# An adaLN transformer block on one core: attention outputs written straight to where the projection reads them, head sets in pairs, and a table of moves over the planned order

## The chip, the cores and the metric

One Trainium2 chip, of which the kernel uses one core. The metric is device time in microseconds (us). A core has five engines with an instruction queue each: TensorE (PE, with its weight loads shown apart as PEld), VectorE (DVE), ScalarE (ACT), GpSimd (POOL) and SyncE (SP, which here issues nearly all DMAs).

## The reference

```python
# x [1, 2048, 640], c [1, 640], bf16; 32 heads of 20; F = 1536
mod = (silu(c) @ w_mod).reshape(1, 6, 1, 640)
sa, ca, ga, sb, cb, gb = mod[:, 0], ..., mod[:, 5]
h = layernorm(x) * (1 + ca) + sa
qkv = (h @ wqkv)                       # 640 -> 3 * 640
p = softmax(q @ k.T * 20 ** -0.5)      # 2048 x 2048 for each head
x = x + ga * ((p @ v) @ wo)            # 640 -> 640
h = layernorm(x) * (1 + cb) + sb
x = x + gb * (((h @ w_gate) * (h @ w_up)) @ w_down)
```

## The kernel before

**A planner writes the program.** The Python code creates some thousand tasks (a group of matmuls, one exponential, one DMA, ...), each with its engine, an assumed duration, a priority, the tasks it depends on and the buffers it must acquire. A list scheduler (`Sched`) runs them against assumed costs and so fixes one order for each of the queues of PE, DVE, ACT, POOL and SP. `emit_program` then writes these orders out with semaphores. On the chip nothing is reordered: each engine goes through its list and waits where a semaphore isn't there yet.

**Tiling.** The 2048 queries are cut in 7 chunks (`CHUNKS`: one of 512, six of 256), the 32 heads in 8 sets of 4 (`NSET`). A pair of chunk and set is an *item*. An item's scores are made in *units* of 512 columns, keys on the partitions; there are 2048 units in all. A *score visit* of PE (line 1524, `ps_all<-QT,KT`) makes two units, with matmuls that use one of four 32-row strips of the array each (a head of a set lies on each strip), into a pair of PSUM banks; there are two such pairs of banks. For most units one ACT instruction (line 1561, `PP<-ps_all`, 1024 columns) takes the exponential of both units into a buffer `PP`. For the units that the table `QUADS` names, in fours, DVE makes it from integer operations on the bits of a bf16: line 1585 (`DB<-ps_all`) takes a unit out of PSUM, lines 1617 and 1625 (`DSS<-DB`) make two terms of four units, and their product is made by DVE (line 1622) or by POOL in four pieces (line 1637).

**PV and the end of an item.** The PV matmuls (line 2192, `ps_all<-PP,Vf` and `<-DSS,Vf`, 128x32 column strips, one strip for each head) sum an item's output in one PSUM bank, 21 columns a head: the sum of the exponentials and 20 outputs. When an item is through, line 1717 (DVE) transposes the bank in 32x32 blocks into `OT`, line 1723 (DVE) takes reciprocals into `invT`, line 1725 (POOL, for the last sets DVE) multiplies, all 32 columns of each head's band, into `OTn`, line 1734 (DVE) transposes back into `OcT`, and strip DMAs of line 1746 on SP (248 issues, 10 KB each as a rule) copy the 20 rows of each head from their bands of 32 to where the output projection wants them, `Ocp` (640 rows as five blocks of 128). The last set of the last chunk is projected from `OcT` itself, with a small copy of its part of w_o, `wo7`.

**The rest of a chunk** is its *suffix*: output projection, residual and LN2, then for each of 12 blocks of 128 of F a gate and an up product (line 970, `ps_all<-h2T,stg`; their weights are loaded anew for each chunk into buffers `stg`) that share one bank, 256 columns each, a copy of the gate half to `gsb` (line 1959; ACT or DVE), the product of both (line 1997, `hprod`), and the down-projection (line 970, `ps_all<-wd,hprod`). The suffix of a chunk is woven between the scores of the next ones, its places set by fractions (`GATE_F`). Fill matmuls (line 2523) stand where PE's planned work is thin.

**The start.** LayerNorm, transposes (copies at line 1133) and the projections to Q, K and V. K and Q go out to DRAM and come back in the layout with one head per 32-row strip: line 1289 (`KT<-k_rows`) and line 1298 (`QT<-q_rows`), on SP. w_o comes early in one DMA, `wo7` in four (line 1493). The later sets' K and Q are projected during the first sets' scores.

The end of an item, cut to the operations:

```python
t1: e.transpose(OT[:, 0:n], ps[:, bank, 0:n]...)                      # DVE, line 1717
t2: e.reciprocal(invT[:, 0:nb32]..., OT[...][:, :, 0:1])              # DVE, line 1723
t3: e.tensor_tensor(OTn[:, 0:n]..., OT[:, 0:n]..., invT..., ALU.mult) # POOL or DVE, line 1725
t4: e.transpose(OcT[:, s, 0:n], OTn[:, 0:n])                          # DVE, line 1734
for (b5, s, r0, nr, ro) in pcs:                                       # SP, line 1746
    e.dma_start(Ocp[r0:r0 + nr, slot, b5, qo:qo + n],
                OcT[32 * s + 1 + ro:32 * s + 1 + ro + nr, s_, 0:n])
```

Of the kernel before, what the change touches and what calls it, by code (L numbers as in the profile page):

```python
# [13 lines left out]
SEM = 60.0  # L14
# [4 lines left out]
X_FIRST = 0.0  # L19
ACT_LAT = 250.0  # L20
# [16 lines left out]
LKTOL = 300.0  # L37


class Task:  # L40
    __slots__ = ("head", "hval", "hknow", "eng", "dur", "lat", "deps", "emits", "ctr", "prio", "gate", "acq", "on_start", "slots",
                 "start", "done", "needed", "val", "know", "nleft", "ready", "users", "name", "mode", "seq", "rt", "sem",
                 "nbytes", "cond", "alt", "land", "firm", "lk", "dead", "key")

    def __init__(self, eng, dur, emits, deps=(), ctr=None, prio=0.0, lat=None, gate=0, acq=(), on_start=None,
# [28 lines left out]
        self.dead = False  # L74
        if lat is None:
            lat = {"pe": PE_DRAIN, "act": ACT_LAT, "dve": DVE_LAT, "pool": 60.0}.get(eng, 0.0)
        self.lat = lat

# [5 lines left out]
class Slots:  # L84

    def __init__(self, ids, name=""):
        self.name = name
        self.free = [(i, []) for i in ids]
        self.hold = {}
        self.gone = set()  # L90
        self.out = {}

    def avail(self, only=None):
        best = None
        for k, (i, rel) in enumerate(self.free):
            if only is not None and i != only:
                continue
            t = 0.0
            for r in rel:
                t = max(t, r.done + SEM)  # L100
            if best is None or t < best[0]:
                best = (t, k)
        return best
# [13 lines left out]
    def done(self, i, task):  # L117
        h = self.hold[i]
# [9 lines left out]
    def add(self, i, rel):  # L128
        self.free.append((i, rel))


class Sched:

    def __init__(self):
# [28 lines left out]
        self.lk_last = None  # L163

# [39 lines left out]
    def _enable(self, task):  # L204
        t = 0.0
        for d in task.deps:
            t = max(t, d.done + SEM)
# [70 lines left out]
    def step_engine(self, eng):  # L278
        if self.free_at[eng] > self.t:
            return False  # L280
        self.pull(eng)
        rl = self.readyl[eng]
        for k, task in enumerate(rl):
# [5 lines left out]
            if self.locked(eng, task):  # L289
                continue  # L290
            if self.acquire(task, self.t):
# [63 lines left out]

def emit_program(nc, sched, nsem_dma=56):
# [23 lines left out]
    for t in sched.all:  # L380
# [11 lines left out]
        for d in deps:  # L392
            if not (d.nbytes or d.eng != eng or d.eng in ("dve", "pool")):
                continue
            if d.head and eng == "act":
# [85 lines left out]
QUADS = ((0, 4, 3, 3, 3, 4, 4, 4), (2, 2, 1, 2, 2, 2, 1, 2), (2, 2, 1, 2, 2, 2, 1, 2), (2, 2, 1, 2, 2, 2, 1, 2), (2, 2, 1, 2, 2, 2, 1, 2), (2, 2, 1, 2, 2, 2, 1, 2), (2, 1, 2, 2, 2, 1, 2, 0))  # L481
SPLITJ = 1
QHALF = ((0, 0), (0, 0))
TB_GATE = 2
# [3 lines left out]
D_LEAD = 0.451  # L488
NB0, NSS = 3, 3
XB0, XSS = 0, 0  # L490
HEADG = 1000
OP_EARLY = 1
EV_OP = 0.5
# [3 lines left out]
LN2T = 0.6  # L497
# [5 lines left out]
HOLD = 110  # L503
PVTOL = 249
XDPRIO = 1.343
# [5 lines left out]
STX_G, STX_T, STX_S, W_ISSUE = 3, 20, 1.5, 600.0  # L511
ZFILL = 1
WD_POOL, WD_PRIO = 1, 400.0
# [4 lines left out]
WM_GATE = 8  # L518
# [3 lines left out]
K_LEAD = 0.683  # L522
# [3 lines left out]
D_LATE = 16  # L526
D_RES = 20
PVMIN, PVMAX, PVCAP = 2, 7, 12
PV0 = 0
V_PARTS = [[0, 2], [2, 4], [4, 6], [6, 8]]  # L530
V_L1 = 0.2
# [10 lines left out]
GATE_F = (0.446, 0.5, 0.5, 0.5, 0.5, 0.5, 1.0)  # L542
FILL_MIN = 4190.746
# [9 lines left out]
LN2P = 0.85  # L553
NALT = 1
OPFIRST = 1500
STG_B = 0.95
ENDP, END3, P_POW = 0.4, 1, -1.0
HT_L = 0.25
V_L = 0.221
LATE_A = 2.065  # L560
LATE_L = 1.418
LATEQ = (2, 3)
LATEQ_A = -20
LATEQ_F = 0.35
# [4 lines left out]
    0: {"PVMIN": 2, "HOLD": 95, "PVTOL": 249, "D_RES": 58, "PVCAP": 6, "X_HALF": 0.0, "XDPRIO": 1.343, "FILL_MIN": 3463.3, "LKTOL": 300.0, "EAGER": 9, "PVMAX": 14, "X_LATE": -179.96, "TPRIO": 0.75, "STEAL_GAP": 200, "D_LATE": 16, "PV_KEEP": 2},  # L569
    1: {"PVCAP": 15, "XBACK": 1, "FILL_MIN": 4629.7},  # L570
    2: {"DL": 0.376},
    4: {"HOLD": 58.0, "X_LATE": -39.3},
    5: {"D_LATE": 7, "PVMAX": 3},
    6: {"X_LATE": 168.4, "FILL_MIN": 5225.9, "HOLD": 156.4},
    7: {"DL": 0.501},
    8: {"FILL_MIN": 2868.8},
    10: {"X_HALF": 69.3, "HOLD": 73.7, "PVMAX": 5},
    11: {"DL": 0.443},
    12: {"DL": 0.459, "HOLD": 108.3, "X_LATE": 6.6},
    13: {"DL": 0.417},  # L580
    15: {"X_LATE": 86.8},
    16: {"HOLD": 135.0, "FILL_MIN": 4362.5},
    17: {"X_LATE": -17.4, "LKTOL": 338.9, "HOLD": 52.0},
    19: {"DL": 0.471, "PVMAX": 7, "HOLD": 113.6},
    20: {"DL": 0.391, "PVMAX": 10},
    21: {"X_LATE": -85.4, "PVMIN": 3},
    24: {"DL": 0.464, "STEAL_GAP": 210.6, "X_LATE": -52.5, "PVCAP": 14, "HOLD": 116.4, "LKTOL": 98.1},
    25: {"DL": 0.549, "LKTOL": 370.4, "HOLD": 156.3},
    26: {"DL": 0.411, "PVMIN": 1, "X_LATE": 2.0, "EAGER": 6, "X_HALF": 58.0},
    27: {"DL": 0.473},  # L590
    29: {"HOLD": 148.6, "D_LATE": 5, "LKTOL": 267.5, "D_RES": 36, "PVMAX": 3},
    30: {"EAGER": 11},
    31: {"X_LATE": -99.6, "HOLD": 173.2, "X_HALF": 164.9, "PV_KEEP": 2},
    33: {"DL": 0.442, "PVMIN": 7, "PV_KEEP": 3, "X_HALF": 147.4},
    34: {"PVMIN": 3, "X_HALF": 26.9, "STEAL_GAP": 91.8, "EAGER": 8, "X_LATE": 136.8, "D_RES": 25},
    35: {"X_HALF": 148.7},
    36: {"DL": 0.524},
    37: {"FILL_MIN": 4112.0, "EAGER": 8, "X_LATE": -201.5},
    39: {"STEAL_GAP": 162.9, "EAGER": 9},
    42: {"PVMAX": 8, "FILL_MIN": 4334.4, "PV_KEEP": 3},  # L600
    43: {"HOLD": 127.6},
    46: {"D_LATE": 20, "PV_KEEP": 3, "X_LATE": -80.9},
    53: {"LKTOL": 820.1, "X_HALF": 73.5},
    54: {"PVTOL": 279.6, "FILL_MIN": 4011.5, "X_HALF": 31.3},
}
XHALF = 1
STG_G0, STG_G, XC_G = 12, -10, -20
X_LATE = -24.052
X_HALF = 0.0
# [10 lines left out]
def build_kernel(nc, A_x, A_wqkv, A_wo, B_x, B_w_gate, B_w_up, B_w_down, c, w_mod, out):  # L620
# [96 lines left out]

    PPs = [alloc("PP", [128, NPS, w * 512], BF16) for w in ((3, 2) if HEADG < 1000 else (2, 2))]
    wo7 = alloc("wo7", [128, D], BF16)
# [9 lines left out]
    OTn = alloc("OTn", [128, 512], BF16)  # L729
    NOC = 2  # L730
    OcT = alloc("OcT", [128, NOC, 512], BF16)
    oc_off = region(2 * KD * 512 * 2)
    Ocp = at("Ocp", [128, 2, KD, 512], BF16, oc_off)
# [6 lines left out]
    late_off = region(late_size)  # L740
    early_off = region(early_size)
    R1 = Sub(late_off, late_size)
# [4 lines left out]
    R1 = Sub(early_off, early_size)  # L747
# [5 lines left out]
    R2 = Sub(early_off, early_size)  # L753
    hprod = R2.alloc("hprod", [128, FT, 512], BF16)
    h2T = R2.alloc("h2T", [128, KD, 512], BF16)
    xck = R2.alloc("xck", [128, 4, D], BF16)
    xn2 = R2.alloc("xn2", [128, 4, D], BF16)
# [8 lines left out]
    KPB = alloc("KPB", [128, 2, 512], BF16)  # L766
# [30 lines left out]
    G = Slots([5, 6, 2, 7], "G")  # L797
    GX = Slots([3, 4] if HEADG else [2, 3, 4], "GX")
    hx = (1, 3) if HEADG else (1, 3, 4)
    GC = Slots([0, 1], "GC")  # L800
    setA = Slots([0], "A")
    setB = Slots([0], "B")
    pPs = [Slots(list(range(NPS)), "PP") for _ in range(2)]

    def ring():
        return len(pPs[0].free) + len(pPs[1].free)
# [3 lines left out]
    sOcT = Slots(list(range(NOC)), "OcT")  # L810
# [407 lines left out]
    def k_base(tc):  # L1218
        return 80 if tc in K_DIRECT else 0
# [87 lines left out]
    def v_round(t, pt, prio, gate=0):  # L1307
        a, z = V_PARTS[pt]
        nh = 4 * (z - a)
        w = nh * DH  # L1310
        mms = []
        for k in range(KD):
            f = quarters(w, lambda k=k: hT[t // 4][:, k, t % 4 * 128:t % 4 * 128 + 128],
                         lambda k=k: wV[:, k, 80 * a:80 * a + w], k == 0, k == KD - 1)
            mms.append((X(w), f))

        def after(r):
            dst = Vf[:, (t * H + 4 * a) * VW:(t * H + 4 * a + nh) * VW].rearrange("p (h w) -> p h w", w=VW)[:, :, 1:VW]
            f = lambda e: e.tensor_copy(dst, ps[:, r.b["b"], 0:w].rearrange("p (h w) -> p h w", w=DH))
# [1309 lines left out]
```

## Time and profile before

| | |
|---|---|
| median of 3 runs | 804.14 us (803.36 to 807.19) |
| profiled execution: span | 803.8 us (0.3 under the median) |
| first exponential starts, last one starts | 16.35 us, 774.7 us |
| DMA over the span | 64.66 MB, mean 80 GB/s |

The profile is one execution of the program, recorded by the hardware; times in it are microseconds from the start of its span. "L1561" is line 1561 of the kernel. A group's row reads: line, engine, operation, output <- inputs, partitions x elements, number of instructions, then busy time, mean ns of one, idle time of the engine before them and what ended it. A row of a wait reads: who waited, on what, for whom, total us, number of waits, longest wait. Matmuls are pipelined and their ends are modelled, so PE's busy time isn't PE at its peak.

### The profile page before, as it was taken

What the parts mean: (1) busy time and instruction counts of PE and PEld (TensorE: products, weight loads), DVE (VectorE), ACT (ScalarE), POOL (GpSimd) and SP (SyncE); (2) the same over time, 40 slices, a digit from 0 to 9 for tenths busy, and PEclk for the clock granted to TensorE, in tenths of its full rate; (3) what the DMA queues carried; (4) which work ended last, traced back from release to release, by engine and by line L of the source; (5) the groups of instructions that cost most, each with busy time, mean ns of one, the idle gap of its engine ahead of it and who ended that gap; (6) DMA issues with size and microseconds to landing.
All of it is one profiled execution on the core that took longest, in us unless ns stands there. A gap on an engine that the chain in (4) does not pass through costs nothing.

```text
span 803.8 us, 37761 instructions
## 1 busy us (share of the span) xinstructions
PE 790.4 (98%) x16595; PEld 380.6 (47%) x16595; DVE 697.8 (87%) x1401; ACT 764.8 (95%) x847; POOL 386.0 (48%) x396
## 2 busy tenths in 40 slices
PE   8999999999999999999999999999999999999998
PEld 4433433333244434445555455555555555555567
DVE  7978788799989999988999999999899988898754
ACT  6899899999999999999999999999999999999961
POOL 3347455654366565763444443545534554455300
PEclk9999999999999999999999999999999999999999
DMA  9733212212341532120032404231540254414420
GB/s 297 243 113 91 62 43 64 61 33 76 92 109 50 167 88 52 35 55 13 24 81 65 95 16 112 57 73 39 121 89 15 54 118 94 98 37 106 92 68 18
DMA packets 154314, 64.66 MB, mean 80 GB/s; under 512 B 116951, under 2 KB 154151, under 8 KB 154151
## 3 DMA queue, kind: packets, MB, share of 16 engines
q1 hardware_dynamic: 153223, 61.10, 30.0%
q8 instruction: 132, 2.16, 1.1%
q10 hardware_dynamic: 928, 1.15, 0.5%
q14 instruction: 31, 0.25, 0.1%
HBM read 50.63 MB, written 8.99 MB: 74 GB/s over the span
## 4 chain that ended last, share of the span: by engine, by line
PE 77%; ACT 14%; DVE 5%; issue 2%; DMA 1%; SPq 1%; POOL 0%; DVEq 0%; ACTq 0%
PE ps_all L1524 26%; PE ps_all L970 21%; PE ps_all L2192 19%; ACT PP L1561 14%; PE ps_all L1230 4%; PE ps_all L966 3%; DVE DB L1585 2%; PE ps_all L1889 1%; PE ps_all L1166 1%; PE ps_all L1127 1%; DVE DSS L1617 1%; PE ps_all L2523 0%; DVE DSS L1625 0%; DMA QT<-q_rows 0%; PE ps_all L991 0%
## 5 line engine op out<-in xcount | busy, mean ns | idle before, releaser
L1561 ACT ACTIVATE PP<-ps_all 128x1024 bf16<-128x1024 f32 x810 | 748.5, 1090 | 6.7 <-PE ps_all L1524 4.8
L1637 POOL TENSOR_TENSOR DSS<-DB,DSS 128x512 bf16<-128x512 bf16 x268 | 305.0, 1157 | 290.6 <-DVE DSS L1625 254.2
L1585 DVE TENSOR_SCALAR DB<-ps_all 128x512 int16<-128x512 f32 x428 | 285.5, 681 | 50.5 <-PE ps_all L1524 48.0
L1524 PE MATMUL ps_all<-QT,KT 32*128 32x256 bf16 (+2 forms) x3648 | 319.4, 287 | 4.5 <-DMA QT<-q_rows 0.8
L1524 PEld LDWEIGHTS ps_all<-QT,KT 32*128 32x128 bf16 x3648 | 93.9, 92 | 204.1 <-ACT PP L1561 141.5
L2192 PE MATMUL ps_all<-PP,Vf 128*32 128x256 bf16 (+2 forms) x2892 | 163.6, 291 | 0.5 <-DVE KPB L1242 0.3
L970 PE MATMUL ps_all<-h2T,stg 128*32 128x256 bf16 (+2 forms) x2716 | 122.9, 281 | 0.3 <-DVE DB L1585 0.2
L2192 PEld LDWEIGHTS ps_all<-PP,Vf 128*32 128x32 bf16 (+1 forms) x2892 | 54.5, 94 | 76.4 <-issue 67.6
L2192 PE MATMUL ps_all<-DSS,Vf 128*32 128x256 bf16 (+1 forms) x1512 | 88.7, 291 | 0.0
L1617 DVE TENSOR_SCALAR DSS<-DB 128x2048 int16<-128x2048 int16 x107 | 77.2, 722 | 0.8
L970 PEld LDWEIGHTS ps_all<-h2T,stg 128*32 128x32 bf16 x2716 | 61.6, 96 | 26.9 <-issue 22.0
L1625 DVE TENSOR_SCALAR DSS<-DB 128x2048 int16<-128x2048 int16 x107 | 73.2, 684 | 0.8 <-PE ps_all L2192 0.8
L970 PE MATMUL ps_all<-wd,hprod 128*32 128x320 bf16 (+1 forms) x1404 | 61.0, 277 | 0.0
L1725 POOL TENSOR_TENSOR OTn<-OT,invT 128x256 bf16<-128x256 f32 (+1 forms) x49 | 35.3, 721 | 37.7 <-DVE invT L1723 37.5
L1622 DVE TENSOR_TENSOR DSS<-DB,DSS 128x2048 bf16<-128x2048 bf16 x40 | 51.5, 1287 | 0.0
L2192 PEld LDWEIGHTS ps_all<-DSS,Vf 128*32 128x32 bf16 x1512 | 36.5, 95 | 20.9 <-issue 12.4
L970 PE MATMUL ps_all<-wV,hT 128*32 128x160 bf16 x1280 | 38.9, 236 | 0.9 <-DVE DB L1585 0.3
L970 PEld LDWEIGHTS ps_all<-wd,hprod 128*32 128x32 bf16 x1404 | 31.2, 96 | 14.2 <-issue 10.8
L1717 DVE STREAM_TRANSPOSE OT<-ps_all 128x256 f32<-128x256 f32 (+2 forms) x57 | 27.1, 475 | 8.8 <-PE ps_all L2192 8.5
L1230 PE MATMUL ps_all<-hT,wk 128*32 128x512 bf16 x360 | 32.3, 382 | 0.0
L970 PEld LDWEIGHTS ps_all<-wV,hT 128*32 128x32 bf16 x1280 | 24.6, 97 | 15.9 <-issue 8.2
L1230 PE MATMUL ps_all<-hT,wq 128*32 128x512 bf16 x375 | 31.3, 382 | 0.6 <-DVE OT L1717 0.6
(133 smaller groups left out, 556.1 us busy)
## 6 DMA issues: line engine op xcount, KB each, us to landing
stg<-in_B_w_gate_dram SPq DMA_DIRECT2D x74, 160.0 KB
stg<-in_B_w_up_dram SPq DMA_DIRECT2D x74, 160.0 KB
KT<-k_rows SPq DMA_DIRECT2D x112, 32.0 KB
QT<-q_rows SPq DMA_DIRECT2D x48, 64.0 KB
Ocp<-OcT SPq DMA_DIRECT2D x164, 10.0 KB
wm<-in_w_mod_dram SPq DMA_DIRECT2D x3, 800.0 KB
x<-in_A_x_dram SPq DMA_DIRECT2D x7, 320.0 KB
k_rows<-KPA SPq DMA_DIRECT2D x16, 128.0 KB
```

The costliest lines, as they stand in the source:

```text
L970: return lambda e, b: e.matmul(ps[32 * x:32 * x + 32, b, c0 + o:c0 + o + w], lhs()[:, 32 * x:32 * x + 32], rhs() if w == n else rhs()[:, o ...
L1230: f = [lambda e, b_, k=k, x=x: e.matmul(ps[x:x + min(32, w - x), b_, :], wx[:, k, r0 + x:r0 + min(x + 32, w)], hT[tc][:, k, :], tile_posit ...
L1524: ems.append(lambda e, i=i, kt=kt: e.matmul(dstf()[:, i * u.n:(i + 1) * u.n], KT[32 * u.s:32 * u.s + 32, u.j, kt * 128:(kt + 1) * 128], QT ...
L1561: return e.activation(PPs[g % 2][:, cellp["p"], 0:nu * 512], ps[:, b0:b0 + nu, :].rearrange("p b c -> p (b c)"), AFT.Exp, scale=ESCALE)
L1585: return e.tensor_scalar(DBl[st_["slot"]][:, x * 512:(x + 1) * 512], bank(cell["b"]), EBIAS, 0.0, op0=ALU.add, op1=ALU.max)
L1617: return e.tensor_scalar(DSl[st_["ss"][0]][:, :], DBl[st_["slot"]][:, :], 0x7F, 0x3F00, op0=ALU.bitwise_and, op1=ALU.bitwise_or)
L1622: return e.tensor_tensor(d, DBl[st_["slot"]][:, :].bitcast(BF16), d, ALU.mult)
L1625: return e.tensor_scalar(DSl[st_["ss"][1]][:, :], DBl[st_["slot"]][:, :], 0x7F80, 2, op0=ALU.bitwise_and, op1=ALU.bitwise_or)
L1637: return e.tensor_tensor(d, DBl[st_["slot"]][:, x * w:x * w + w].bitcast(BF16), d, ALU.mult)
L1717: t1 = Task("dve", n * 1.1 + 70, lambda e: e.transpose(OT[:, 0:n], ps[:, item_info[it]["bank"], 0:n].rearrange("p (b q r) -> p b r q", q=3 ...
L1725: f3 = lambda e: e.tensor_tensor(OTn[:, 0:n].rearrange("p (b c r) -> p b r c", c=32, r=2), OT[:, 0:n].rearrange("p (b r c) -> p b r c", c= ...
L2192: ems.append(lambda e, i=i, kt=kt, stt=stt, stp=stp: e.matmul(ps[32 * s:32 * s + mc, bk, 0:u.n], Vf[:, (kt * H + 4 * u.j + s) * VW:(kt * H ...
```

## The change

1. **Outputs straight to `Ocp`.** The multiply keeps 20 columns of each head, not 32, and puts them beside each other in a buffer `OTn` that holds the outputs of all eight sets of a chunk, so that the 160 columns of a partition group fill five bands of 32. The second transpose then goes from `OTn` to `Ocp`, for those bands that the set has filled. `OcT`, the 248 strip DMAs and `wo7` are gone. Since each strip of `Ocp` now holds the heads in another order, the rows of w_o are permuted, by 48 DMAs of 4 to 20 rows (line 1898 of the changed kernel) in place of one and four.
2. **Pairs.** For chunks of 256 queries two head sets (even and odd) share one PSUM bank in PV, 256 columns each; lines 1717 and 1723 then run once for both, over 512 columns.
3. **Gate and up.** A bank holds two gate blocks or two up blocks, not one of each: the copy to `gsb` and the product run over 512 columns, half as often. Two more `stg` buffers (`MORE = 2`).
4. **Score visits.** Which units share a visit is chosen while the planner runs, among the next six (`LOOK = 6`), so that they lie on different strips; `PP` is one ring of 16 slots, and the exponential may write two slots that don't lie side by side (a strided output, 464 of them, `128x2x512`).
5. **The planner.** Its costs have new latency terms (`LAT_X`, `REL_X`, `V_X`, `S_X`), and the tables are new ones: `QUADS` has 109 fours for 107, the gates of the suffix differ (`GATE_F`, and a table of its stages).
6. **A table of moves.** When the planner is done, `replan` takes 1810 tasks out of their places in the orders and puts them into others (1311 on PE, 314 on SP, 162 on DVE, 22 on POOL, 1 on ACT; the median move is 6 places on PE and 17 on SP), and then runs the new orders against the assumed costs once more to date the tasks.

The core of the diff:

```diff
-        f3 = lambda e: e.tensor_tensor(
-            OTn[:, 0:n].rearrange("p (b c r) -> p b r c", c=32, r=2),
-            OT[:, 0:n].rearrange("p (b r c) -> p b r c", c=32, r=2),
-            invT[:, 0:nb32]....to_broadcast([128, nb32 // 2, 2, 32]), ALU.mult)
+        def f3(x):
+            return lambda e: e.tensor_tensor(
+                OTn[:, g0:g0 + gn, DH * (j + x):DH * (j + x) + DH, :].rearrange("p b c r -> p b r c"),
+                OT[:, nq_ * x:nq_ * x + nq_].rearrange("p (b r c) -> p b r c", c=32, r=2)[:, :, :, 1:1 + DH],
+                invT[:, 2 * gn * x:2 * gn * (x + 1)]....to_broadcast([128, gn, 2, DH]), ALU.mult)
...
-        t4 = dve(n * .55 + 65, lambda e: e.transpose(OcT[:, cell["s"], 0:n].bitcast(F32), OTn[:, 0:n].bitcast(F32)), [t3],
...
-                return e.dma_start(Ocp[r0:r0 + nr, slot, b5, qo:qo + n],
-                                   OcT[32 * s + 1 + ro:32 * s + 1 + ro + nr, cell["s"], 0:n])
+            def f4(e):
+                o = Ocp[slot][:, b0:b1, qo:qo + nq_].bitcast(F32).rearrange("p k (b c) -> p k b c", c=32)
+                i = OTn[:, g0:g0 + gn, 32 * b0:32 * b1, :].rearrange("p b (k c) r -> p k b (c r)", c=32).bitcast(F32)
...
+                return e.transpose(o, i)
...
-    d_wo = [dma("sp", 128 * KD * D * 2, lambda e: e.dma_start(wo_sb[:, :, :], wov[:, :, :]), [d_wm[3][0]], prio=10)]
+    for j in range(NSET):
+        i0 = DH * j
+        while i0 < DH * j + DH:
+            i1 = min(DH * j + DH, i0 // 32 * 32 + 32)
+            for x in range(4):
+                def fwo(e, x=x, i0=i0, i1=i1, j=j):
+                    r0 = 4 * DH * j + DH * x + i0 - DH * j
+                    p0 = 32 * x + i0 % 32
+                    return e.dma_start(wo_sb[p0:p0 + i1 - i0, i0 // 32, :], A_wo[r0:r0 + i1 - i0, :])
...
+            if n <= 256 and GU2:
+                two.append((wbuf, dm))
+                if fc % 2 == 0:
+                    continue
...
+                            f = lambda e: e.tensor_copy(gsb[:, gs, 0:2 * n], ps[:, r.b["b"], 0:2 * n])
...
+def replan(sc):
+    for eng, moves in PLAN.items():
+        old = sc.order[eng]
+        gone = {a for a, _ in moves}
+        new = [t for i, t in enumerate(old) if i not in gone]
+        for a, b in moves:
+            new.insert(b, old[a])
+        sc.order[eng] = new
...
```

More of the change, by code (lines that the diff above doesn't have):

```diff
@@ L2137, in pv_candidates @@
                     break
+            elif it in lead and any(first_pv[(lead[it], s)] for s in range(4)):
+                break
             na = 0
@@ L2250, in pv_issue @@
         for it in sorted(last):
-            if item_info[it]["left"] == 0:
-                t1 = t1s[it]
-                t1.deps = [last[it]]
+            o = own(it)
+            if all(item_info[x]["left"] == 0 for x in (o, second.get(o, o))) and not t1s[o].firm:
+                t1 = t1s[o]
+                t1.firm = True
+                t1.deps = [max(last.values(), key=lambda x: x.done)]
                 sc.left -= 1
@@ L2389, in d_attach @@
             dst["next"] += 1
-            n += 1
-        return n
+        elif not MON[0]:
+            d_attach(ts, t, ap - nu + EAGER, rows, 2, False)
+        if us and len(ts.emits) > nh:
+            ts.head = nh
+            ts.hfor = ta
+        dur = 216.0 * max(rows.values()) * clk() + S_X.get(len(ts.emits), 0.0)
+        sc.activity(start, 128.0 * sum(rows.values()))
+        sc.left += 1
+        sc.finish_issue(ts, start, dur)
+        if us:
+            sc.add(ta)
+        pvstate["sidx"] += 1
```

914 lines of the change are left out of this document (601 added, 313 removed), and 202 rows, old and new, of the table PLAN.

## The prediction

> **What bounds the kernel now.** I read the page first, then busy time by stage, then the waits, then the order of time on two engines.
>
> ```profile
> span 803.8 us, 37761 instructions
> PE 790.4 (98%) x16595; PEld 380.6 (47%) x16595; DVE 697.8 (87%) x1401; ACT 764.8 (95%) x847; POOL 386.0 (48%) x396
> ```
>
> PE and ACT are both nearly full, and DVE is close. The stages, cut at the first exponential (16.35 us), the 80th (99.5), the 800th (766.4) and the last (774.7); the sixth row is the best stretch I found:
>
> ```profile
> 0.00:16.35 16.35, 13.65 (x178) 6.56 (x182) 11.08 (x46) 10.18 (x22) 4.86 (x15) 1.00 0.95 306
> 16.35:99.50 83.15, 81.11 (x1448) 34.54 (x1440) 68.24 (x154) 76.58 (x86) 42.73 (x51) 0.98 0.48 135
> 99.50:766.40 666.90, 661.21 (x14396) 313.00 (x14399) 599.86 (x1150) 664.48 (x721) 337.24 (x328) 1.00 0.29 71
> 766.40:774.70 8.30, 8.18 (x200) 4.57 (x189) 2.55 (x8) 8.30 (x11) 0.00 (x0) 1.00 0.29 65
> 774.70:803.80 29.10, 26.22 (x408) 21.96 (x405) 16.08 (x46) 5.22 (x13) 1.14 (x2) 0.99 0.06 19
> 375.48:393.57 18.09, 17.92 (x418) 9.11 (x410) 16.84 (x28) 18.09 (x22) 6.75 (x7) 1.00 0.05 14
> ```
>
> Columns: stretch, its length, then busy time and instructions of PE, weight loads, DVE, ACT, POOL, then clock, DMA share, GB/s. In the sixth row the exponentials start every 18.08/20 = 0.904 us (the 22 include one cut at each edge). That is ACT's floor for one: 720 of them cost 650.9 us, and the third row took 666.9, so ACT loses 16.0 us there although it looks 99.6% busy.
>
> Is PE the reason? Its busy time counts the modelled end of each matmul, so I price its work by start times:
>
> ```profile
> 560.22 0.41 PE L2192 MATMUL ps_all<-PP,Vf 128*32 128x256 bf16 x8
> 560.45 0.40 PE L970 MATMUL ps_all<-h2T,stg 128*32 128x256 bf16 x8
> 560.78 0.40 PE L1524 MATMUL ps_all<-QT,KT 32*128 32x256 bf16 x6
> 561.11 0.29 PE L970 MATMUL ps_all<-h2T,stg 128*32 128x256 bf16 x4
> 561.40 0.39 PE L1524 MATMUL ps_all<-QT,KT 32*128 32x256 bf16 x4
> 561.72 0.73 PE L970 MATMUL ps_all<-h2T,stg 128*32 128x256 bf16 x20
> 562.38 0.39 PE L1524 MATMUL ps_all<-QT,KT 32*128 32x256 bf16 x4
> ```
>
> Four matmuls of 256 columns, one per strip of the array, cost 0.107 us together: the twenty at 561.72 take 0.66 up to the next row, five such groups and one change of array shape. Eight followed by eight of the same shape take 0.23 (560.22 to 560.45): 0.214 and a seam of 0.016. Eight followed by a score visit (another shape) take 0.33, so a change of shape costs 0.116; the visit of four at 561.40 takes 0.32, 0.213 and 0.107. I use 0.115. Summed over the kernel's own order of instructions: columns 579.0 us, 1652 changes of shape 190, 367 seams 6, together 775 of 803.8. By the same prices the stretch of the third row holds 650.6 us of PE work, against ACT's 650.9 and the measured 666.9. So two engines with equal work hand each other banks, and each loses 16 us. The waits confirm that PE hardly waits for anyone else:
>
> ```profile
> PEld ps_all L1524 <- ACT PP L1561: 141.5, 479, 1.3
> DVE DB L1585 <- PE ps_all L1524: 48.0, 90, 2.0
> ACT PP L1561 <- PE ps_all L1524: 4.8, 12, 0.8
> ```
>
> The first row is score weights loaded ahead of a bank that the exponential still reads; most of it is covered by matmuls of other lines. DVE waits for PE, not PE for DVE.
>
> **The change, part by part.**
>
> *Score units.* The QUADS table gives DVE 109 quads for 107. Counted in the two built orders: 806 exponentials for 810, 4 x 0.904 = 3.6 us less ACT, and 8 more line 1585 operations for DVE. The strided output (128x2x512, 464 of them) has no row in this trace; the columns are the same, so between 0 and, at a tenth, 0.09 us each; I take 0.
>
> *PE.* Counted in the built orders: changes of shape 1652 to 1592, -60 x 0.115 = -6.9 us; seams 367 to 176, -191 x 0.016 = -3.1; columns 579.0 to 580.0, +1.0. Sum -9.0. By place, with the same prices: the first 80 exponentials 80.6 us before and after; the next 720, 650.6 to 642.8, -7.8; the rest nearly equal. The seams go because gate and up rounds and the outputs of a pair of head sets now share a bank, so longer runs stay together; the shape changes go because the moved order joins visits (12 double visits in that stretch, 3 before).
>
> *The end.* PE work behind the last score visit grows from 24.2 to 27.8 us of columns (down-projection matmuls that stood earlier now stand there, 3.6 us), just what four fewer exponentials save. Those two cancel, and the last two stages keep 37.4 us together.
>
> *DVE and POOL.*
>
> ```profile
> L1637 POOL TENSOR_TENSOR DSS<-DB,DSS 128x512 bf16<-128x512 bf16 x268 | 305.0, 1157 | 290.6 <-DVE DSS L1625 254.2 <-DVE DSS L1622 22.0 <-DVE xn L1851 8.2
> L1622 DVE TENSOR_TENSOR DSS<-DB,DSS 128x2048 bf16<-128x2048 bf16 x40 | 51.5, 1287 | 0.0
> L1959 DVE CAST gsb<-ps_all 128x256 bf16<-128x256 f32 x60 | 24.6, 412 | 4.7 <-PE ps_all L970 4.6
> L1997 DVE TENSOR_TENSOR hprod<-ps_all,gsb 128x512 bf16<-128x512 f32 x12 | 8.1, 677 | 0.4 <-PE ps_all L970 0.4
> L1717 DVE STREAM_TRANSPOSE OT<-ps_all 128x256 f32<-128x256 f32 x47 | 20.8, 442 | 4.8 <-PE ps_all L2192 4.7
> L1717 DVE STREAM_TRANSPOSE OT<-ps_all 128x512 f32<-128x512 f32 x8 | 5.7, 712 | 1.4 <-PE ps_all L2192 1.3
> L1734 DVE STREAM_TRANSPOSE OcT<-OTn 128x128 f32<-128x128 f32 x47 | 14.2, 301 | 1.5 <-POOL OTn L1725 1.5
> L1725 POOL TENSOR_TENSOR OTn<-OT,invT 128x256 bf16<-128x256 f32 x42 | 27.9, 665 | 37.2 <-DVE invT L1723 37.0
> ```
>
> Gate copies and products: 120 of 256 columns at 0.412 become 60 of 512 at 0.677, 49.4 to 40.6, -8.8. Transposes of the outputs: 46 x 0.442 become 23 x 0.712, -3.9. The second transposes: 57 (17.6 us and more) become 31 of like sizes (about 10.5), -7. Five quads' products go to POOL, -5 x 1.287 = -6.4. More score units and their terms, about +8. Reciprocals, about -3. DVE falls by some 21 of 698 us. POOL gains 28 x 1.14 = 32 and loses about 13 where 32 columns of each head become 20; at 48% busy that is covered, by idle time that waits for DVE. ACT takes three more line 1133 copies (0.77 each) among its first exponentials, in a stage where it idles 6.6 us of 83.15. I cost DVE's saving at nothing: PE waits little for it.
>
> *Queues.* The 248 strip DMAs into Ocp (line 1746) go; the transpose writes Ocp itself. Nothing waited long for them. The permuted w_o comes in 48 small DMAs in place of 5, all on SP in the first set's 16 to 110 us, between the loads of K.
>
> ```profile
> 66.74 9.55 SPq L1289 DMA_DIRECT2D KT<-k_rows  x16
> 87.61 2.98 SPq L1746 DMA_DIRECT2D Ocp<-OcT  x4
> 90.71 0.92 SPq L1298 DMA_DIRECT2D QT<-q_rows  x2
> 94.31 0.40 PE L1524 MATMUL ps_all<-QT,KT 32*128 32x512 bf16 x4 [0.82 <-DMA QT<-q_rows]
> 33.12 1.75 SPq L1493 DMA_DIRECT2D wo<-in_A_wo_dram  x2
> 35.33 0.34 SPq L1493 DMA_DIRECT2D wo<-in_A_wo_dram  x1
> ```
>
> An issue takes 0.34 to 0.88 us; 48 at 0.5 are 24 us, less some nine Ocp issues at 0.75 that leave this stage. The rows show that SP's queue can hurt: two Q loads stood behind four Ocp issues, and PE then waited 0.82 us. In the new order one w_o piece stands there. Bounds: -1 us (that wait gone) to +23 (rival three); I take 0, for SP waits long at other places of this stage.
>
> **The sum.** Start 0, first 80 exponentials 0, the next 720 -7.8 (PE's saving passed on whole, which the floor of ACT allows up to -16.0), end 0: 803.8 - 7.8 = 796.0, and with the 0.3 us by which the median of the runs (804.14) lies over this span, **796.3 us**. About 0.5% (4 us) is what a measurement of this kernel can tell from no change.
>
> **Rivals.** *One: ACT is the bound, and PE's relief is hidden.* For it: exponentials are the only group that runs all through, and PE's weights wait for them 141.5 us. Against: ACT loses 16 us in the stretch, and 20 in a row lose nothing where PE is in time. Then only the exponentials count, their saving is eaten at the end, and the time is 804 less at most 1 or 2: 803. [...]
>
> *Two: the moved order also heals the hand-over.* Of the 16.0 us, 8.2 are left after my sum; if two thirds go, as the sixth row shows possible, and 2 of the first 80's 2.5 over PE's 80.6, the time is 796.3 - 5.5 - 2 = 789.
>
> *Three, slower: K rows come late behind w_o on SP.* Seven later sets need their K, and 48 pieces are 6 to 7 per set, 3.3 us. If more than half of that is uncovered, the scores of each set stall, ACT with them: 7 x 1.7 to 7 x 3.3 is 12 to 23 us; at 14, 796.3 + 14 = 810. It decides from about 0.6 us a set uncovered, where it eats the gain. For it: the wait at 94.31. Against: SP also has idle spans, and only some sets' loads are tight.
>
> *Four: the clock.*
>
> ```profile
> 93.00:96.00 3.00, 2.00 (x44) 0.76 (x41) 1.22 (x3) 2.38 (x4) 3.00 (x4) 1.00 0.62 144
> 97.00:100.50 3.50, 3.50 (x56) 1.21 (x46) 1.97 (x4) 2.74 (x3) 0.00 (x0) 0.53 0.02 5
> ```
>
> After a stretch with PE a third idle, the granted clock was about half for 3.4 us: 1.7 us of work lost. A PE with 1.2% more slack and 152 fill matmuls for 168 may see it more often; six more such stretches cost 10 us: 806. [...]
>
> **Chances.** Forecast 0.43 (its own range 792 to 800), one 0.22 (800 to 805), two 0.20 (785 to 792), three 0.10, four 0.05. Faster by over 0.5% is below 800.1: 0.42 of the forecast, 0.01 of one and 0.19 of two, 0.62. Slower by over 0.5%, above 808.2: three and a third of four with a remnant of one, 0.12. Same: 0.26. The range 786 to 808 leaves out a sixth: most of three, the lowest of two.
>
> **What would show it.** Right: 806 exponentials, their mean pitch in the middle stretch down from 0.925 to about 0.915, first exponential near 16.4, last start to end about 32.7 us (29.1 before), DVE near 677 us. Rival one: pitch still 0.925. Two: below 0.910. Three: first 80 exponentials over 86 us with PE waits for KT loads. Four: more rows of half clock. I would be wrong at the root if PE's priced work fell as counted and the span rose without any of these.

## The result, and the profile after

The changed kernel takes 815.17 us (median of 4 runs, 813.29 to 818.55), the kernel before 804.46 beside it: 1.0129 times the time, 95% interval 1.0099 to 1.0158. The forecast was 796.3.

The page of the changed kernel, its head, its busy time, the clock in 40 slices, and the group of the exponentials:

```profile
span 816.8 us, 37498 instructions
PE 794.1 (97%) x16648; PEld 376.9 (46%) x16648; DVE 695.6 (85%) x1276; ACT 760.9 (93%) x847; POOL 417.0 (51%) x416
...
PEclk9997999999999999999999999999999999999999
...
L2909 ACT ACTIVATE PP<-ps_all 128x1024 bf16<-128x1024 f32 x806 | 742.9, 1143 | 18.3 <-PE ps_all L1929 12.3
```

Before, ACT waited 4.8 us for score banks; now 12.3, in 20 waits, and the clock row has a 7 in its fourth slice (61 to 82 us). The stages, cut at the first exponential, the 80th, the 800th, and from the last one on (the last two rows cut the middle one at the 500th):

```profile
0.00:17.20 17.20, 14.60 (x183) 7.16 (x187) 10.96 (x46) 9.92 (x22) 4.86 (x15) 1.00 0.81 263
17.20:110.50 93.30, 87.10 (x1516) 35.67 (x1504) 71.63 (x156) 79.05 (x90) 39.06 (x45) 0.93 0.42 117
110.50:778.50 668.00, 658.15 (x14331) 305.93 (x14327) 590.38 (x1018) 661.81 (x721) 367.93 (x351) 1.00 0.28 68
...
783.60:816.80 33.20, 29.67 (x518) 25.44 (x518) 18.27 (x52) 5.41 (x14) 1.56 (x3) 1.00 0.14 37
110.50:497.90 387.40, 381.81 (x7525) 161.57 (x7521) 342.45 (x596) 385.96 (x422) 222.51 (x211) 1.00 0.24 62
497.90:778.50 280.60, 276.34 (x6818) 144.35 (x6810) 247.93 (x423) 275.85 (x301) 145.41 (x140) 1.00 0.34 76
```

For the kernel before, the middle stage cut at the same exponential:

```profile
99.50:490.00 390.50, 386.80 (x7674) 166.50 (x7677) 356.06 (x661) 388.46 (x421) 207.20 (x198) 1.00 0.25 65
490.00:766.40 276.40, 274.42 (x6730) 146.50 (x6726) 243.80 (x490) 276.02 (x301) 130.04 (x131) 1.00 0.35 79
```

The span is 13.0 us longer: 0.85 before the first exponential, 10.15 in the first 80, -3.1 up to the 500th, +4.2 up to the 800th, -3.2 to the last one (four fewer), +4.1 behind it. From the 80th to the 800th the mean pitch of the exponentials is 0.928 us, for 0.926 before and 0.915 forecast. Where the first 80 lost it, in the changed kernel, by stretches:

```profile
22.00:24.00 2.00, 0.34 (x2) 0.04 (x2) 0.27 (x1) 1.72 (x2) 0.00 (x0) 1.00 0.05 18
24.50:28.00 3.50, 3.27 (x30) 1.41 (x34) 3.50 (x11) 1.02 (x1) 0.88 (x3) 0.55 0.77 211
62.00:65.00 3.00, 0.98 (x14) 0.22 (x12) 1.09 (x3) 1.50 (x2) 0.00 (x0) 1.00 0.32 96
65.00:76.00 11.00, 11.00 (x106) 2.85 (x105) 7.17 (x11) 8.08 (x8) 5.84 (x4) 0.54 0.38 96
```

Two stretches with PE idle, each followed by the half clock: 3.4 us of it after the first, ten after the second. What PE waited for stands in the chain of work that ended last (start, length, what) and in the waits between 60 and 66 us:

```profile
17.52 6.19 DMA x<-in_A_x_dram
...
23.73 0.49 DVE st L1444
...
59.59 0.45 SPq L1662
...
60.54 0.42 SPq L1898
...
61.38 0.97 SPq L1662
...
62.85 1.79 DMA KT<-k_rows
...
64.69 0.40 PE ps_all L1929 x4
```
```profile
PE ps_all L1929 <- DMA KT<-k_rows: 2.0, 1, 2.0
```

First x came late, then one set's K rows (line 1662), behind a row of other issues on SP. From 57 us on, four of these are w_o (line 1898); they take 1.8 us, against the wait of 2.0. The order of x on SP's queue, in the changed kernel and in the kernel before:

```profile
11.62 4.96 SPq L1230 DMA_DIRECT2D x<-in_A_x_dram  x2
17.11 0.37 SPq L1241 DMA_DIRECT2D wk<-in_A_wqkv_dram  x1
17.52 0.54 SPq L1230 DMA_DIRECT2D x<-in_A_x_dram  x1
23.73 0.37 SPq L1241 DMA_DIRECT2D wq<-in_A_wqkv_dram  x1
24.14 0.53 SPq L1230 DMA_DIRECT2D x<-in_A_x_dram  x1
```
```profile
11.70 3.58 SPq L857 DMA_DIRECT2D x<-in_A_x_dram  x4
```

In the program each early load waits for an earlier one to land: in the first 30 us the loads of the QKV weights waited 9.6 us on SP for x to land, and 2.4 before. Before, the waited-for one stands four places ahead, and four x loads are issued within 3.6 us, the last before 15.3 us. The table of moves put wk and wq between them: now wk waits for the x two places ahead, wq for the x right ahead of it, and the last x, queued behind wq, is issued at 24.1 us.

The four runs differ in this: their mean granted clocks are 1.000 (813.29 us), 1.000 (814.61), 0.998 (815.74) and 0.992 (818.55, the profiled one). So the half clock of the rows above belongs to this execution; with the clock at 1.000 the change still costs 9 to 10 us.

### The profile page after: what moved, and what is told of

Same layout as the page of the kernel before. It is cut to its first block, busy times and chain, and to the rows that moved or that the text cites. A ratio compares the mean times of both kernels' runs of the same rounds, so it can differ in the third digit from the quotient of the medians.

```text
span 816.8 us, 37498 instructions
## 1 busy us (share of the span) xinstructions
PE 794.1 (97%) x16648; PEld 376.9 (46%) x16648; DVE 695.6 (85%) x1276; ACT 760.9 (93%) x847; POOL 417.0 (51%) x416
## 4 chain that ended last, share of the span: by engine, by line
PE 50%; ACT 29%; DMA 6%; DVE 5%; issue 5%; SPq 3%; POOL 2%; ACTq 0%
ACT PP L2909 29%; PE ps_all L1929 18%; PE ps_all L1343 15%; PE ps_all L2609 11%; PE ps_all L1603 3%; DMA x<-in_A_x_dram 2%; PE ps_all L1339 2%; DVE DB L1956 2%; POOL DSS L2012 2%; SPq L2296 1%; DVE DSS L1992 1%; DMA stg<-in_B_w_up_dram 1%; DVE DSS L2000 1%; PE ps_all L3072 1%; DMA stx<-in_B_w_gate_dram 1%
## 5 line engine op out<-in xcount | busy, mean ns | idle before, releaser
L2909 ACT ACTIVATE PP<-ps_all 128x1024 bf16<-128x1024 f32 x806 | 742.9, 1143 | 18.3 <-PE ps_all L1929 12.3
L2012 POOL TENSOR_TENSOR DSS<-DB,DSS 128x512 bf16<-128x512 bf16 x296 | 348.2, 1201 | 289.5 <-DVE DSS L2000 242.7
L1929 PEld LDWEIGHTS ps_all<-QT,KT 32*128 32x128 bf16 x3648 | 94.0, 92 | 219.4 <-ACT PP L2909 179.8
L2609 PE MATMUL ps_all<-PP,Vf 128*32 128x256 bf16 (+3 forms) x2876 | 161.7, 289 | 0.0
L2609 PE MATMUL ps_all<-DSS,Vf 128*32 128x256 bf16 (+3 forms) x1544 | 96.2, 291 | 1.2 <-POOL DSS L2012 1.1
L2609 PEld LDWEIGHTS ps_all<-PP,Vf 128*32 128x32 bf16 (+1 forms) x2876 | 67.8, 95 | 45.2 <-issue 38.2
L1992 DVE TENSOR_SCALAR DSS<-DB 128x2048 int16<-128x2048 int16 x109 | 81.6, 748 | 3.6 <-PE ps_all L2609 2.2
L2000 DVE TENSOR_SCALAR DSS<-DB 128x2048 int16<-128x2048 int16 x109 | 76.3, 700 | 0.8 <-PE ps_all L2609 0.5
L2609 PEld LDWEIGHTS ps_all<-DSS,Vf 128*32 128x32 bf16 (+1 forms) x1544 | 41.5, 96 | 20.3 <-issue 13.2
L1997 DVE TENSOR_TENSOR DSS<-DB,DSS 128x2048 bf16<-128x2048 bf16 x35 | 44.4, 1267 | 0.3
L2094 POOL TENSOR_TENSOR OTn<-OT,invT 128x160 bf16<-128x160 f32 (+1 forms) x44 | 24.9, 584 | 23.5 <-DVE invT L2089 23.5
L1603 PE MATMUL ps_all<-hT,wk 128*32 128x512 bf16 (+1 forms) x360 | 32.2, 399 | 0.1
L1343 PE MATMUL ps_all<-wo,Ocp 128*32 128x320 bf16 (+1 forms) x660 | 28.6, 282 | 0.0
```

The lines of the kernel that those rows point to most:

```text
L1343: return lambda e, b: e.matmul(ps[32 * x:32 * x + 32, b, c0 + o:c0 + o + w], lhs()[:, 32 * x:32 * x + 32], rhs() if w == n else rhs()[:, o ...
L1603: f = [lambda e, b_, k=k, x=x: e.matmul(ps[x:x + min(32, w - x), b_, :], wx[:, k, r0 + x:r0 + min(x + 32, w)], hT[tc][:, k, :], tile_posit ...
L1929: ems.append(lambda e, i=i, kt=kt: e.matmul(dstf()[:, i * u.n:(i + 1) * u.n], KT[32 * u.s:32 * u.s + 32, u.j, kt * 128:(kt + 1) * 128], QT ...
L1992: return e.tensor_scalar(DSl[st_["ss"][0]][:, :], DBl[st_["slot"]][:, :], 0x7F, 0x3F00, op0=ALU.bitwise_and, op1=ALU.bitwise_or)
L1997: return e.tensor_tensor(d, DBl[st_["slot"]][:, :].bitcast(BF16), d, ALU.mult)
L2000: return e.tensor_scalar(DSl[st_["ss"][1]][:, :], DBl[st_["slot"]][:, :], 0x7F80, 2, op0=ALU.bitwise_and, op1=ALU.bitwise_or)
```

## The experiments

**The table emptied** (`PLAN` without moves).

> The table of 1810 moves is emptied; all else is the changed kernel. Theory A (the moves of the SP queue cost the time, the PE moves gain some): by the prices of the prediction PE's work goes from 769 back to 776 us, so the middle stretch loses again what it gained (about 3 us between exponentials 80 and 500), but the first 80 exponentials, which took 93.3 us against 83.2 before, come back to 84 to 86; the time is 803 to 808. Theory B (the new structure costs it: 48 loads of w_o on SP, strided exponentials, pairs): the first 80 stay above 90 us and the time stays at 812 to 818.

Measured: 808.21 us (1.0047 of before, 1.0033 to 1.0061). Its stages, for the first 80 exponentials, up to the 500th, up to the 800th, and behind the last:

```profile
17.00:102.70 85.70, 83.14 (x1516) 35.84 (x1504) 72.32 (x160) 77.80 (x89) 37.00 (x45) 1.00 0.46 126
102.70:489.40 386.70, 383.17 (x7540) 164.83 (x7533) 332.25 (x591) 385.53 (x422) 217.53 (x211) 1.00 0.24 62
489.40:767.70 278.30, 276.64 (x6794) 147.80 (x6786) 245.21 (x424) 275.39 (x301) 138.09 (x140) 1.00 0.34 77
772.20:805.20 33.00, 30.10 (x538) 25.75 (x538) 18.28 (x52) 5.57 (x14) 2.23 (x4) 1.00 0.07 22
```

The moves cost 7 us (6.6 by the ratios, which set each kernel beside its own runs of the kernel before). And on PE they gain nothing: without them PE's work, counted in the built order at the prediction's prices, is 376.2 us between the 80th and the 500th exponential, with them 373.5, but the stretch is 386.7 here and 387.4 with them. That part of theory A, a loss of 3 us, was wrong.

**SP's moves alone taken out** (the key "sp" of `PLAN` left out).

> Only the 314 moves of the SP queue are taken out; those of PE, DVE, POOL and ACT stay. Theory A: the first 80 exponentials at 84 to 87 us, the steady pitch of the changed kernel kept, no late gate or up weights near 745 us; the time is 796 to 803, so the rest of the change is worth 2 to 8 us over the kernel before. Theory B: 812 or more. Rival C (the moved PE order needs the moved SP order, since it asks for K and Q rows in another order): PE waits for KT and QT in the first 200 us, over 820.

Measured: 811.16 us (1.0075, 1.0057 to 1.0094). Neither theory; rival C in its kind, at a smaller price. PE waits once for K rows, and the clock is at half from 59.9 us on, inside that wait:

```profile
PE ps_all L1931 <- DMA KT<-k_rows: 3.4, 1, 3.4
```
```profile
52.90 4.59 SPq L1900 DMA_DIRECT2D wo<-in_A_wo_dram  x7
57.53 1.98 SPq L1664 DMA_DIRECT2D KT<-k_rows  x4
```
```profile
60.00:73.00 13.00, 11.87 (x106) 2.97 (x109) 7.27 (x11) 8.01 (x8) 5.85 (x4) 0.50 0.50 119
```

Here K does stand behind seven pieces of w_o, 4.59 us. The moved PE order asks for K where the planner's SP order is not ready with it.

**The first 17 places of SP put back.** The edit stands in `replan`:

```diff
         sc.order[eng] = new
+        if eng == "sp":
+            at = {id(t): i for i, t in enumerate(old)}
+            new[:17] = sorted(new[:17], key=lambda t: at[id(t)])
```

> All moves stay, but the first 17 places of SP's queue (loads of c, x, the QKV weights and the first modulation weights) are put back in the planner's order, which has three chained loads in flight where the moved order has at times one. Theory A in its narrow form (these places alone make the late start): the first exponential at 16.3 to 16.6 us, the 20th at 40 to 42 us (46.0 in the changed kernel, 40.2 before), about 5 us less in all, 809 to 811; the wait for K rows at 62 us and the half clock behind it may stay. If the 48 pieces of w_o are the whole cost: 814 to 816.

Measured: 811.22 us (1.0089, 1.0067 to 1.0112), 3 to 4 us less than the changed kernel; first exponential at 16.9, the 20th behind it at 41.1 us. The first 80 take 85.1 us. PE still waits 2.4 us for K rows in two places among them, but in the profiled execution no half clock follows. Between the 500th and the 800th it still takes 281.5 us:

```profile
490.00:771.50 281.50, 276.52 (x6822) 144.52 (x6814) 248.10 (x423) 276.04 (x302) 145.37 (x140) 1.00 0.34 76
```

**The first 60 places put back** (60 for 17 in the edit above).

> As the run before, but with the first 60 places of SP's queue put back in the planner's order among themselves (the first K and Q rows, the modulation weights, the first pieces of w_o). Theory A: also the wait of 2.5 us for K rows at 62 us and the ten us of half clock after it go; the first 80 exponentials take 84 to 87 us and the time is 803 to 807. If the half clock comes from PE's own order and not from the wait, it stays and the time is 808 to 811.

Measured: 811.63 us (1.0086, 1.0066 to 1.0106), nothing gained over 17, so theory A's 803 to 807 was missed. The waits for K are gone from the first 80 exponentials; in the profiled execution PE waits 0.3 us for Q rows, and the clock is 0.50 from 76.5 to 79.5 us and, late, from 745.5 to 748.5.

**w_o in one piece, late** (on the kernel without moves: its 48 tasks put behind SP's 88th place, the multiplications later on DVE).

> As the kernel without the table of moves, but the 48 loads of w_o stand in one piece on SP's queue, behind its 88th place (after about 112 us), and the five multiplications of w_o by the gate on DVE after about 150 us. Theory A2 (the w_o pieces between the loads of K and Q make the first 80 exponentials 2.5 us longer than before, 85.7 for 83.2): the first 80 take 83 to 84.5 us, the time is 806 to 807.5. If SP is covered there: 808, no change.

Measured: 826.80 us (1.0259, 1.0231 to 1.0287). A miss, and a useful one. The first 80 exponentials took 85.1 us for 85.7, so the w_o pieces among them cost 0.6 us at most, not 2.5. But where the 48 stand now, K was due:

```profile
108.63 18.68 SPq L1912 DMA_DIRECT2D wo<-in_A_wo_dram  x48
...
127.79 1.76 SPq L1676 DMA_DIRECT2D KT<-k_rows  x4
```
```profile
PE ps_all L1943 <- DMA KT<-k_rows: 13.3, 1, 13.3
```
```profile
120.50:140.50 20.00, 9.49 (x95) 2.63 (x95) 4.41 (x8) 6.14 (x6) 0.00 (x0) 0.50 0.25 64
```

0.39 us an issue, 18.7 in all, 13.3 of it uncovered, and 20 us of half clock.

**The old costs** (`LAT_X`, `REL_X`, `S_X` empty, `V_X` zero), **no pairs** (`PAIRS = 0`) and **gate and up in one bank** (`GU2 = 0`), each on the kernel without moves.

> As the kernel without the table of moves, but the planner's new latency and cost terms (LAT_X, REL_X, V_X, S_X) are emptied, so that it plans with costs like those before; the structure stays. Theory D (the gain between exponentials 80 and 500, 10.8 us above the floor before and 7.0 without the moves, comes from better placed PE work, at nearly the same sum of PE work): that excess goes back to 9.5 to 12 us and the time is 811 to 818. Rival (the gain comes from pairs, wider gate and up rounds, the one ring of buffers): the excess stays at 6.5 to 8.

> As the kernel without the table of moves, but each head set has its own PV bank and its own transposes and reciprocal (PAIRS = 0). The prediction's term for this edit was some 7 us of DVE and seams of PE, costed at nothing on DVE. If pairs carry the gain between exponentials 80 and 500: the excess there goes from 7.0 to 9 us or more. If DVE's saving is covered, as predicted: 6.5 to 8 there, and a time within 4 us of 808; the planner places 224 more fill matmuls in this plan, which lie in gaps.

> As the kernel without the table of moves, but gate and up share a bank again, 256 columns each (GU2 = 0), so copies to gsb and products are twice as many and half as long, 8.8 us more on DVE by the prediction. If DVE's saving there is what the gain between exponentials 80 and 500 comes from: excess 9 us or more. If it is covered: 6.5 to 8 us, and a time within 4 us of 808.

Measured: 832.24, 821.66 and 828.19 us (1.0318, 1.0188 and 1.0268). In all three PE waits 2 to 3 us for K rows in the first 80 exponentials, with half clock behind it, and their ends take 38.6 to 39.6 us for the 33.0 without moves; the planner's tables were made for another plan, so the totals, which missed what was expected, say little of the edits. The question was the stretch from the 80th to the 500th exponential. Its time above 420 x 0.904 us, before the change 10.8 and without the moves 7.0, is 8.6 with the old costs, 7.4 without pairs, 6.6 without the wider rounds. So pairs and wider rounds do not carry that gain. The cost terms carry part of it: pitches of 0.93 to 1.20 us make 6.6 us of the loss before, 3.1 without the moves and 5.9 with the old costs. The sum, 8.6, stayed under the 9.5 expected. Theory D took the sum of PE work to be nearly the same; over the whole kernel it is, but not in this stretch, as the table behind the last two runs shows.

**Fill matmuls at the K wait** (nine groups ahead of score visit 37 of the changed kernel).

> The changed kernel with all its moves, and nine fill matmul groups (each four matmuls of 512 columns of the identity, 0.21 us together) on PE ahead of score visit 37, the one that waits for K rows at 62 us; they write a PSUM bank that is free at that time, and give nothing to the output. Theory E (the wait itself costs 2 us, the idle PE in it costs the clock, and the clock the rest: about half of full speed from 65 to 76 us, 5 us of work): the wait for K rows stays, the clock stays at 1.00 behind it, the first 80 exponentials take 87 to 89 us for 93.3 and the time is 809 to 812. Rival (the clock falls for another reason, or its fall is hidden by waits): the time stays at 813 to 816.

Measured: 816.57 us (1.0140, 1.0106 to 1.0174), no less. In its profiled execution the clock had fallen at 57 us already, so the fills ran at half of it; behind them, from 65 us, it was 1.00 throughout, and it fell again from 174 to 184 us. Two of its runs with mean clock 1.000 took 812.2 and 814.3 us, those of the changed kernel 813.3 and 814.6. So neither side is shown; what is shown is that the half clock comes and goes between runs (the mean clocks of these six are 0.990 to 1.000) and isn't the bulk of the 10.7 us.

**The first 17 places of SP and those from the 400th on put back.**

> The changed kernel with the first 17 places of SP's queue and those from the 400th on put back in the planner's order among themselves; all other moves stay. In the moved order the weights of the last chunk (stx, used behind the last scores) stand ahead of gate and up weights (stg) that PE waits for at 744 to 750 us. Theory A: these two stretches are what the SP moves cost; the excess between exponentials 500 and 800, 10.3 us with the first 17 places alone put back, falls to 7 to 8.5, and the time is 807.5 to 809.5. If the late stretch costs by PE's order and not by SP's: 811.

Measured: 808.07 us (1.0029, 1.0013 to 1.0045), as theory A had it, and 3.2 us less than with the 17 alone (4.8 by the ratios). Between the 500th and the 800th exponential:

```profile
490.30:769.20 278.90, 276.39 (x6810) 144.59 (x6802) 248.32 (x423) 275.67 (x301) 145.41 (x140) 1.00 0.35 78
```

The late cause can be read from SP's queue; the changed kernel, then this one:

```profile
740.24 1.09 SPq L2296 DMA_DIRECT2D stx<-in_B_w_gate_dram  x2
...
742.52 1.27 SPq L2296 DMA_DIRECT2D stx<-in_B_w_up_dram  x2
743.83 0.70 SPq L2296 DMA_DIRECT2D stg<-in_B_w_up_dram  x1
```
```profile
740.55 0.94 SPq L2303 DMA_DIRECT2D stg<-in_B_w_gate_dram  x2
```

Weights of the last chunk (`stx`) go in front of those that PE waits for. In the changed kernel PE then stood idle for them, among other places, here:

```profile
745.48 0.40 PE L1343 MATMUL ps_all<-h2Tt,stg 128*32 128x256 bf16 x8 [0.51 <-DMA stg<-in_B_w_gate_dram]
750.21 0.40 PE L1343 MATMUL ps_all<-h2Tt,stg 128*32 128x256 bf16 x8 [1.02 <-DMA stg<-in_B_w_up_dram]
```

Its waits for gate and up weights behind the 500th exponential sum to 2.6 us; in this run no `stx` is issued from 730 to 757.4 us, and the first one stands behind the `stg` of 754.5 and 757.0. Those two stretches, 119 of SP's 502 places, are 7.1 of the 10.7 us (8.0 by the ratios).

**More and less PE work in the kernel before.** The first is a doubling of four matmuls of each gate round, the second leaves a fifth of each gate product out:

```diff
+                        if k == 0 and w_ == 0:
+                            f = f + f
                         mms.append((X(n), f))
```
```diff
-                        mms.append((X(n), f))
+                        mms.append((X(n), [lambda e, *a: None for _ in f] if k == 2 and w_ == 0 else f))
```

> The kernel before, its orders unchanged, but the first four matmuls of each gate round are issued twice (the second time over the first, with the same result): 240 matmuls more, 5.8 us of PE work by the prediction's prices, nearly all between exponentials 80 and 800. The prediction's step (PE's work is passed on whole in the middle stretch): the time rises by 5 to 6.5 us. Rival one of the prediction (ACT sets the pace, PE's work is hidden): it rises by 0 to 2 us.

> The kernel before with the third of the five contraction blocks of each gate round left out (the gate product is a sum over four fifths of the features): 256 matmuls less, 6.5 us less PE work by the prediction's prices between exponentials 80 and 800 (1.5 of it before the 500th); the plan moves slightly with it (8 fill matmuls more). The prediction's step (what PE saves in the middle stretch is passed on whole): the time falls by 5 to 7 us, to 798 to 800. Rival one of the prediction (ACT's pace hides it): it falls by 0 to 1.5 us. In between, 2 to 4.5 us: near the balance of the two engines a saving is passed on in part, as the added work of the run before was (3.2 of 5.8).

Measured: with more, 808.32 us beside 805.12 (1.0045, 1.0027 to 1.0062); with less, 804.31 beside 804.98 (0.9995, 0.9981 to 1.0009). The first lies between the two expectations, the second is what rival one expected. The added 240 matmuls are 60 groups of four, at 0.107 us 6.4 us and not 5.8; half of that was passed on. From the 500th to the 800th exponential, with more and with less:

```profile
489.50:769.30 279.80, 278.51 (x6912) 151.37 (x6914) 244.62 (x490) 279.20 (x301) 129.89 (x131) 1.00 0.35 78
```
```profile
487.20:763.10 275.90, 272.20 (x6514) 141.49 (x6510) 243.32 (x489) 275.76 (x301) 134.25 (x135) 1.00 0.35 80
```

After the 500th exponential, where 5 us of work were added, the stretch grew from 276.4 to 279.8; where 5 were taken out, it became 275.9. So there PE's work is passed on in large part when it grows, and hardly when it shrinks. What it saves becomes a longer wait for ACT, in the row that the prediction read as covered (141.5 us before); with more work, with less, and in the changed kernel:

```profile
PEld ps_all L1524 <- ACT PP L1561: 118.2, 371, 1.1
```
```profile
PEld ps_all L1524 <- ACT PP L1561: 158.4, 548, 0.8
```
```profile
PEld ps_all L1929 <- ACT PP L2909: 179.8, 638, 1.1
```

Before the 500th exponential it is otherwise. There 1.6 us more made the stretch 1.3 us longer, and 1.6 less made it 0.8 shorter. The run with less also lost 1.5 us behind the last exponential, where PE now waits for the LN2 output:

```profile
778.87 1.90 PE L966 MATMUL ps_all<-h2Tc,stx 128*128 128x128 bf16 x31 [1.14 <-DVE h2Tc L1879]
```

The kernels side by side suggest where the line lies. PE's work is counted here in the built orders at the prediction's prices for columns and changes of shape, without the seams, and placed by the start times of each profile; the second number is the time of the stretch above ACT's floor (0.904 us for each exponential).

| | PE work, 80th to 500th | above the floor of 379.7 | PE work, 500th to 800th | above the floor of 271.2 |
|---|---|---|---|---|
| before, more PE | 379.3 | 12.1 | 271.8 | 8.6 |
| before | 377.7 | 10.8 | 267.0 | 5.3 |
| before, less PE | 376.1 | 10.0 | 262.1 | 4.7 |
| old costs | 375.4 | 8.6 | 269.7 | 11.2 |
| no moves | 373.0 | 7.0 | 268.9 | 7.1 |
| no wider rounds | 372.2 | 6.6 | 271.3 | 16.3 |
| changed | 370.9 | 7.7 | 268.0 | 9.5 |
| no pairs | 369.3 | 7.4 | 271.6 | 13.2 |

Up to the 500th exponential the loss falls with PE's work, 5.1 us for 6.3, until that work is some 7 us under ACT's floor; below 373 us nothing more is gained. After the 500th the kernel before has that slack already. There the last five kernels lose more at nearly the same work, since ACT waits 2.4 to 10.8 us for `PP` slots, and the changed kernel for weights too. The runs with the changed kernel's PE order that are left out have its 370.9 us and lose 7.1 to 9.0 up to the 500th (11.4 with a spell of half clock in it). So the gain up to the 500th goes with PE's work in that stretch. This is a reading of single executions; no run was made to test it by itself.

None of the twelve beats the kernel before.

## Why the prediction was wrong

- **"PE's saving passed on whole", -7.8 us.** This step of the sum failed. The count may stand, but less than half of the saving reached the time: 3.1 us up to the 500th exponential in the changed kernel, and 3.8 without any moved PE order. In the kernel before, 6.5 us less PE work gave 0.7 us less, within its interval of -1.5 to +0.7. The prediction set 650.6 us of PE work against 650.9 of ACT over the whole stretch, and took the 16 us that both lose for something that any saving of PE would heal. By the table, which suggests this but does not prove it, the saving lies before the 500th exponential, where it is passed on until PE has some 2% less work than ACT, and not below; after the 500th PE was that far below ACT from the start. What PE saves beyond that is waited for ACT, in the row of 141.5 us (179.8 in the changed kernel). Rival one, to which this row spoke, was right for that part; that PE's work is hidden altogether isn't so either, for half of the added work came through.
- **The queues, "bounds -1 to +23; I take 0".** This term, put at nothing, was the decisive one, about +7 us (7.0 by emptying the whole table, 7.1 by putting 119 places of SP back). Rival three named the queue, and its sign came: the first 80 exponentials took 93.3 us, over its 86, with PE waiting for K. But it blamed 48 pieces of w_o in the first 110 us. They were spread up to 209 us in the changed kernel, and cost little in the first 80 exponentials without the moves (0.6 us at most); with them, four stand in front of the late K rows, and seven in the run without SP's moves. Most of the cost lies in the order of the 314 moved SP tasks, which the prediction counted and did not read: x behind loads that wait, K behind other issues, `stx` ahead of `stg`. All three can be seen in the built order alone.
- **Rival four, the clock.** It was right in kind, and bigger than "1.7 us a stretch": one spell was 10.2 us long. By the rows the profiled execution lost 11 x 0.46 + 3.5 x 0.45 = 6.6 us of PE's speed to it, against 3.5 x 0.47 = 1.6 before. Two of the four runs had none (mean clock 1.000), so it isn't the median's main term. In the long spell PE was busy in 11.00 of 11.00 us at 0.54, as the profile counts it, with modelled ends; what gives the full clock back no run shows.
- **Right:** 806 exponentials; the end, from 29.1 to 33.2 us (32.7 forecast), just eating the exponentials' saving; strided exponentials at no cost (the median pitch behind the 464 strided ones is 0.904 us, as behind the other 341).
- **DVE at 677 us:** 682.5 without the moves, 695.6 with them. DVE's busy time fell by 15 us of the 21 counted; what was not foreseen is below.
- **Still open:** some 3 to 4 us. Without moves the first 80 exponentials take 2.5 us longer than before, and more beside a kernel before without its spell of half clock (81.4 us in the runs with more and with less PE work). By the count of the table PE has 2.3 us more work there (79.3 for 77.0) and 1.9 more after the 500th: at an equal sum, work moved out of the stretch between. One wait remains between the 500th and the 800th: ACT stands 2.4 us (changed kernel, at 533 us) for `PP` slots whose PV matmuls come late. A plan without that wait wasn't tried.

```profile
ACT PP L2909 <- PE ps_all L2609: 2.4, 1, 2.4
```

## What to carry to other kernels

Two engines with equal work do not mean that either's saving is the kernel's saving: add a little work to one and take a little away, in the stretch where the saving lies, and see which of the two moves the time (here 6.4 us more on PE cost 3.2 us, and 6.5 less took off 0.7). When a change reorders queues, read the new order of each queue for the first thing that each engine waits for, DMAs above all; a count of instructions says nothing of a load that stands behind another that waits. And an order that was only run against assumed costs is to be tried part by part on the chip: here the moves of one queue cost some 7 us.

## What the runs showed of the hardware

- The half clock lasted from 3.4 to 20.5 us, by the clock of the profiled executions: 3.4 us in the kernel before (from 96.9 us), 3.4 and 10.2 in the changed kernel (from 24.8 and 65.8), 6.8 with the fills (from 57.7), 13.6 with SP's moves out (from 59.9) and 20.5 with w_o in one piece (from 120.3). Shortly before each of these PE was idle for a part of the time, not always for all of it: it was busy for 2.00 of the 3 us from 93 in the kernel before, for 0.34 of the 2 us from 22 and 0.98 of the 3 us from 62 in the changed kernel, for 0.51 of the 2 us from 54 with the fills, for 1.73 of the 4 us from 56 with SP's moves out, and not at all in the 2 us from 118 with w_o in one piece. How little work it takes, and what sets the length of a spell, no run shows. With the old costs PE was busy in all of 20.5 us at a clock of 0.51:

```profile
66.50:87.00 20.50, 20.50 (x187) 5.14 (x183) 10.76 (x19) 13.58 (x14) 9.10 (x9) 0.51 0.34 86
```

- The same DVE and POOL instructions took longer in another order. Line 1992's 109 took 748 ns on the mean, and 704 without the moves; POOL's 351 instructions between the 80th and the 800th exponential took 367.9 us, and 355.6 without the moves. What slows them no run shows; the changed kernel:

```profile
L1992 DVE TENSOR_SCALAR DSS<-DB 128x2048 int16<-128x2048 int16 x109 | 81.6, 748 | 3.6 <-PE ps_all L2609 2.2
L2012 POOL TENSOR_TENSOR DSS<-DB,DSS 128x512 bf16<-128x512 bf16 x296 | 348.2, 1201 | 289.5 <-DVE DSS L2000 242.7
```
